# A build-time scheduler gets new prices for transfers and instructions, and its order of all instructions is searched anew

## The chip, the cores and the metric

The kernel runs on one core of a Trainium2 chip. The metric is the device time of one execution in microseconds (us). The median of three runs of the kernel before is 364.08 us (363.77 to 364.1).

## The reference

Block-sparse attention and then a SoLU feed-forward layer, all in float32.

```python
# q, k, v: 4 batches, 8 heads, 768 positions, 64 columns
k_sum = k in blocks of 32, max;  v_sum = v in blocks of 32, mean
scores = [q k^T / 8 where |i-j| < 16, else -1e9 ;  q k_sum^T / 8 + log 32]
a = softmax(scores);  x = a @ [v; v_sum]          # 3072 tokens x 512 (heads side by side)
h = x @ w_in                                      # 512 -> 1024
solu = h * softmax(h);  ln = layernorm(solu) * g
out = ln @ w_out                                  # 1024 -> 512
```

## The kernel before

The 3072 tokens are 24 tiles of 128 (`t`), two to a step of attention (256 positions of one batch, in two halves of four heads each). For one half, `scores` makes score products on TensorE (tile `s`), VectorE adds the mask and takes the maximum (L678), ScalarE makes the exponentials (L686), VectorE or GpSimd scales them (`MUL_E`, tile `e`); `values_turn` transposes them on TensorE (tile `t`) and copies them to `at`; `values` multiplies with the value rows `vt` (tile `x`). Then `first` (tiles 0 to 7) or `first_two` (pairs from tile 8 on, seven products for eight) computes h (tiles `h`, `hu`, `hl`, `hf`), `solu` the activation, and `second_parts` the last product (tile `o`, 24 matmuls of 128x128 by 128x512 for each tile). All float32 products are made of three matmuls on rounded high and low parts, so nearly each operand costs VectorE, ScalarE or GpSimd a rounding and a subtraction. The weights arrive as 64-bit floats, and `rounded` turns each of 16 pieces (8 of `w_in`, 8 of `w_out`) into high and low words with five instructions (tile `cv`), the last of them an integer addition (`ADD_W`).

From tile 6 on, the centred rows are transposed by a trip through DRAM: `send` (L1038, L1042: tile `tbl`, one buffer, to `farl`) and `fetch` (L1048: four reads into `lt`).

Nothing is issued where it stands in the code. Each call of `op` hands a `Plan` one operation with its engines (one or a few to choose from), a price on each, what it reads and writes, and for a DMA its bytes. `Plan.order` then simulates the engines at build time: over and over it takes the operation that can begin first, ties by a due number, and puts it on the engine where it ends first. `Plan.issue` runs the operations in that order, and since every engine works its queue in order, this fixes the order on each engine. `SEARCHED` is a list of seeds; each shifts some due numbers or the leaning of some operations to an engine, and the list is what an earlier search kept. A price that differs from the chip's changes nothing but the order.

Two more things come from the plan's clock. Where the plan sees TensorE idle before 80 us (`FILL`), `keep_up` issues matmuls of zeros (L1300), one for each 0.22 us of plan time. And `order` models the port that VectorE and GpSimd share: an operation with `port=True` on VectorE waits in the plan until a GpSimd operation with a port has ended (`lock`), and the other way round (`held`).

A transfer of the plan before has one pipe with a rate by time (`RATES`: 205 GB/s up to 6.9 us, then 420, 365, 410), and lands 0.2 us behind it up to 50 us of plan time and 2.2 us behind it later (`LAND`, `LATE`). The first product with the rows of v for the block means (L546) has `late = LATE_ROWS`, 2.2 us, which is added to its start when zeros are filled in.

Of the kernel before, what the change touches and what calls it, by code (L numbers as in the profile page):

```python
# [17 lines left out]
AF = mybir.ActivationFunctionType  # L18
ALU = mybir.AluOpType
AX = mybir.AxisListType  # L20

P = 128
# [63 lines left out]
class Plan:  # L86
# [6 lines left out]
    RATES = (6.9, 205.0), (30.0, 420.0), (60.0, 365.0), (1e9, 410.0)  # L93
    SMALL, LATE = 40.0, 50.0
    LAND = 2.2
# [8 lines left out]
    SEARCHED = -856134719, -860457018, 52477149, 195803496, 905169564, -371301522, -289478668, -495083861, -295360282,\  # L104
# [145 lines left out]
    def order(self):  # L250

        ready, free, then, dma, held, lock = {}, {}, {}, 0.0, 0.0, 0.0
# [18 lines left out]
        def take(e):  # L271

            if e in then:
                return next(((begin(e, at), o) for at, o in ready[e] if o is then[e]), None)
            best = None
            for at, o in ready[e]:
                t = begin(e, at)
                if any(begin(f, at) + loss(f, o, t) < t + loss(e, o, t) for f in o.can if f != e):
# [7 lines left out]
            for at, y in ready[e]:  # L286
                s = begin(e, at)
# [8 lines left out]
        while len(order) < len(self.ops):  # L296
# [11 lines left out]
            if e == "dve" and o.port:  # L308
                held = o.end
            if e == "pool" and o.port:  # L310
                lock = o.end
            if o.nbytes:
# [3 lines left out]
                o.end = (own if e == "act" else dma) + (0.2 if dma < self.LATE else self.LAND)  # L316
# [19 lines left out]
def attn_then_solu(ctx: ExitStack, tc: tile.TileContext, q, k, v, vr, vb, w_in, w_out, g_ln, out):  # L336
# [11 lines left out]
    COPY_KS = ((pool, 0.35), (dve, 0.19))  # L348
    COPY_P = ((act, 0.48), (dve, 0.6))
    COPY_X = ((act, 0.48), (dve, 0.6))  # L350
    LO_W = ((dve, 0.6), (pool, 1.26))
    ADD_W = ((dve, 0.6), (pool, 1.3))
    MUL_E = ((pool, 1.8), (dve, 1.07))
# [91 lines left out]
    def rounded(key, tag, bufs):  # L445
# [19 lines left out]
        op(act, 0.6, lambda: nc.scalar.activation(  # L465
# [8 lines left out]
        tt(ADD_W, ALU.add, high, high, low, r=[(st, 1)], w=[(st, 0)], port=True)  # L474
# [77 lines left out]
    def mean_values_pe(b):  # L552
# [18 lines left out]
        for g in range(4):  # L571
            op(act, 0.34, lambda g=g: nc.scalar.dma_start(
# [53 lines left out]
    def scores(b, g, pp, direct=False, each=False):  # L626
# [38 lines left out]
        else:  # L665
            yield 2.0 if direct else 1.07, lambda: (mm(0), mm(1)), [(qs, 2 * pp), (qs, 2 * pp + 1)] + ([x, y] if direct else [kw]), [sc]
# [24 lines left out]
        op(act, 0.2, lambda: nc.scalar.activation(out=z.ap, in_=z.ap, func=AF.Copy, bias=1e-9), w=[z])  # L691
        op(dve, 0.1, lambda: nc.vector.reciprocal(out=z.ap, in_=z.ap), w=[z])
# [4 lines left out]
    def run(*parts, rest=True, off=0.0):  # L697
# [18 lines left out]
    def values_turn(b, g, pp):  # L716
# [4 lines left out]
        yield 0.62, lambda: turn_halves(tp.ap[:KC], lambda n: e.ap[:, n, :]), [e], [tp]  # L721
# [5 lines left out]
    def values(b, g, pp, t=NT, apart=False):  # L727
# [36 lines left out]
        yield 2.2 if apart else 1.17, mm, [vs, at] + [vm] * apart, [xb]  # L764
# [19 lines left out]
    def combine(b, g, pp, xb):  # L784
# [19 lines left out]
        half, whole = ((act, 0.34), (dve, 0.33)), ((act, 0.48), (dve, 0.6))  # L804
        lo_h, lo_w = [(dve, 0.33)], [(dve, 0.6)]
        lo_hs, lo_ws = [(dve, 0.33), (pool, 0.7)], [(dve, 0.6), (pool, 1.28)]
        if pp == 0:
# [4 lines left out]
            split(hi, lo, 1, 1, 0, lambda: of(1), [(f, 1)], (((act, 0.34), (dve, 0.2)), lo_hs))  # L812
        else:
# [8 lines left out]
            split(hi2, lo2, 2, 1, 0, lambda: of(2), [(f, 2)], (((act, 0.34), (dve, 0.2)), lo_hs))  # L822
# [79 lines left out]
    def first(t):  # L902
# [5 lines left out]
        for c, nh in sorted(w_in_pieces, key=lambda x: x[::-1]):  # L908
# [7 lines left out]
            op(pe, 0.695, mm, r=[(hi, c), (lo, c), w], w=[hp])  # L916
        solu(t, [(lambda hp=hp: hp.ap, hp) for hp in hs])

    def first_two(t, behind, turns, rest=True):
# [7 lines left out]
        def product(xs, n, w, to, first, after=()):  # L927
            hi, lo = xs
            for c in range(2):
# [5 lines left out]
                op(pe, 0.695, mm, r=[(hi, n), (lo, n), *w(c).keys], w=[to])  # L935
# [41 lines left out]
    def solu(t, hs, maxes=None):  # L977
# [16 lines left out]
        for i, (hp, key) in enumerate(hs):  # L994
            op(act, 0.71, lambda i=i, hp=hp: nc.scalar.activation(  # L995
# [350 lines left out]
```

## Time and profile before

| what | value |
|---|---|
| median of three runs | 364.08 us |
| span of the profiled execution (its own time is not given apart from the span) | 362.6 us |
| TensorE busy (matmul) | 354.2 us, 98% |
| VectorE, ScalarE, GpSimd busy | 84%, 78%, 43% |
| granted TensorE clock | 1.00 through the span |

The span is that of one profiled execution, from its first to its last instruction; the runs take 1.2 to 1.5 us more than it. A busy time of TensorE holds the zeros too, and the ends of matmuls are modelled, so 98% does not say that TensorE computes 98% of the time.

### The profile page before, as it was taken

What the parts mean: (1) busy time and instruction counts of PE and PEld (TensorE: products, weight loads), DVE (VectorE), ACT (ScalarE), POOL (GpSimd) and SP (SyncE); (2) the same over time, 40 slices, a digit from 0 to 9 for tenths busy, and PEclk for the clock granted to TensorE, in tenths of its full rate; (3) what the DMA queues carried; (4) which work ended last, traced back from release to release, by engine and by line L of the source; (5) the groups of instructions that cost most, each with busy time, mean ns of one, the idle gap of its engine ahead of it and who ended that gap; (6) DMA issues with size and microseconds to landing.
All of it is one profiled execution on the core that took longest, in us unless ns stands there. A gap on an engine that the chain in (4) does not pass through costs nothing.

```text
span 362.6 us, 9384 instructions
## 1 busy us (share of the span) xinstructions
PE 354.2 (98%) x3332; PEld 277.0 (76%) x3332; DVE 305.5 (84%) x964; ACT 281.6 (78%) x815; POOL 157.3 (43%) x290
## 2 busy tenths in 40 slices
PE   8999999999999998999999999999999999999995
PEld 3537667768777786788788888888888888888885
DVE  4989999998999999997899999797797996947430
ACT  4888999979869978989698696896796796946320
POOL 6612330166968867423924147350335054534200
PEclk9999999999999999999999999999999999999999
DMA  7999994145325435538489384384164283344611
GB/s 241 413 414 405 359 397 155 62 113 165 130 77 196 136 131 173 172 95 273 141 270 285 117 280 153 114 288 148 57 201 174 55 276 101 116 147 168 209 58 58
DMA packets 28530, 68.19 MB, mean 188 GB/s; under 512 B 3852, under 2 KB 13324, under 8 KB 26948
## 3 DMA queue, kind: packets, MB, share of 16 engines
q1 hardware_dynamic: 24620, 60.87, 49.6%
q10 hardware_dynamic: 3864, 6.74, 5.2%
q8 instruction: 26, 0.43, 0.5%
q14 instruction: 20, 0.16, 0.1%
HBM read 49.55 MB, written 15.73 MB: 180 GB/s over the span
## 4 chain that ended last, share of the span: by engine, by line
PE 63%; DVE 22%; DMA 5%; ACT 3%; SPq 3%; issue 2%; POOL 1%; ACTq 0%; DVEq 0%
PE o L1108 29%; PE hu L932 10%; PE hl L932 5%; PE x L761 4%; PE s L659 3%; PE h L913 3%; DVE e L678 3%; PE t L714 3%; DMA qt<-in_q 2%; DMA farl<-tbl 2%; PE hf L932 2%; DVE e L370 2%; SPq L602 2%; DVE w L489 2%; DVE hm L990 2%
## 5 line engine op out<-in xcount | busy, mean ns | idle before, releaser
L1108 PE MATMUL o<-w,lh 128*128 128x512 f32 (+1 forms) x400 | 128.0, 385 | 0.9 <-DVE w L489 0.9
L1108 PEld LDWEIGHTS o<-w,lh 128*128 128x128 f32 x400 | 74.1, 188 | 16.4 <-DVE w L489 1.2
L1108 PE MATMUL o<-w,ll 128*128 128x512 f32 (+1 forms) x200 | 76.2, 381 | 0.0
L686 ACT ACTIVATE e<-e,nm 128x120 f32<-128x120 f32 x192 | 73.2, 388 | 0.0
L913 PE MATMUL h<-w,xh 128*128 128x512 f32 x128 | 43.0, 400 | 0.0
L1108 PEld LDWEIGHTS o<-w,ll 128*128 128x128 f32 x200 | 37.6, 188 | 6.8
L678 DVE CUSTOM_DVE_ANT_0 e<-s,mask 128x120 f32<-128x120 f32 x192 | 40.6, 276 | 0.5 <-PE s L659 0.3
L686 ACT ACTIVATION_READ_ACCUMULATOR e<-e,nm 128x1 f32 x192 | 37.0, 193 | 0.0
L363 ACT COPY at<-t 120x512 f32<-120x512 f32 x43 | 22.9, 591 | 11.0 <-PE t L714 8.6
L913 PEld LDWEIGHTS h<-w,xh 128*128 128x128 f32 x128 | 24.0, 188 | 7.3 <-ACT at L363 0.8
L1015 ACT ACTIVATE he<-he,nmu 128x512 f32<-128x512 f32 x36 | 24.7, 721 | 4.4 <-DVE nmu L1006 4.3
L761 PEld LDWEIGHTS x<-at,vt 120*64 120x64 f32 (+1 forms) x768 | 24.4, 138 | 4.1 <-issue 2.6
L371 POOL TENSOR_TENSOR ll<-lt,lh 128x512 fp32r<-128x512 f32 x11 | 16.5, 1512 | 23.5 <-DVE lh L364 15.8
L1038 DVE STREAM_TRANSPOSE tbl<-he 128x1024 f32<-128x1024 f32 x18 | 22.3, 1239 | 5.3 <-DMA farl<-tbl 2.7
L1114 ACT ACTIVATE os<-o,y 128x512 f32<-128x512 f32 (+1 forms) x20 | 13.5, 675 | 17.0 <-PE o L1108 16.8
L761 PE MATMUL x<-at,vt 120*64 120x64 f32 (+1 forms) x768 | 26.5, 224 | 0.0
L588 POOL TENSOR_TENSOR st_v<-st_v 96x512 f32<-96x512 f32 (+3 forms) x28 | 22.1, 797 | 8.3 <-DMA st_v<-in_vb 7.8
L1018 ACT ACTIVATE sq<-he 128x1024 bf16<-128x1024 f32 x24 | 25.3, 1056 | 0.1
L913 PE MATMUL h<-w,xl 128*128 128x512 f32 x64 | 25.1, 393 | 0.3 <-DVE xl L770 0.3
L363 ACT CAST lh<-lt 128x512 fp32r<-128x512 f32 x33 | 19.2, 608 | 7.8 <-DMA lt<-farl 5.6
L995 ACT ACTIVATE he<-hs,hm 128x512 f32<-128x512 f32 x24 | 17.1, 716 | 8.3 <-DVE hm L985 8.3
L370 DVE TENSOR_TENSOR e<-e,z 128x960 f32<-128x960 f32 x18 | 23.1, 1281 | 0.1
(175 smaller groups left out, 836.0 us busy)
## 6 DMA issues: line engine op xcount, KB each, us to landing
vt<-in_v SPq DMA_DIRECT2D x12, 1024.0 KB
farl<-tbl SPq DMA_DIRECT2D x18, 512.0 KB
lt<-farl SPq DMA_DIRECT2D x72, 128.0 KB
kraw<-in_k SPq DMA_DIRECT2D x16, 400.0 KB
out<-os ACTq DMA_DIRECT2D x23, 256.0 KB
qt<-in_q SPq DMA_DIRECT2D x11, 512.0 KB
raw<-in_w_in SPq DMA_DIRECT2D x8, 512.0 KB
raw<-in_w_out SPq DMA_DIRECT2D x8, 512.0 KB
```

What stands on the lines that cost most here:

```text
L363: by = {act: lambda: nc.scalar.copy(out=to(), in_=of()), dve: lambda: nc.vector.tensor_copy(out=to(), in_=of()), pool: lambda: nc.gpsimd.t ...
L370: by = {dve: lambda: nc.vector.tensor_tensor(out=to(), in0=a(), in1=b(), op=kind), pool: lambda: nc.gpsimd.tensor_tensor(out=to(), in0=a() ...
L588: op(pool, 0.15 + w * 0.0021, lambda w=w, o=o: nc.gpsimd.tensor_tensor(out=o.ap[:n, :w], in0=x.ap[:n, :w], in1=x.ap[:n, w:2 * w], op=ALU.add),
L678: nc.vector.tensor_tensor_reduce(out=e.ap[:, n, :], in0=sc.ap[:, j, (2 * i + up) * KC:(2 * i + up + 1) * KC], in1=mask[:, mi, :], scale=-S ...
L686: nc.scalar.activation(out=e.ap[:, n, :], in_=e.ap[:, n, :], func=AF.Exp, bias=nm.ap[:, n:n + 1], scale=-1.0, accum_out=z.ap[:, n:n + 1])
L761: nc.tensor.matmul(xp()[j * D:(j + 1) * D, i, qs], vs.ap[:k, u, cs], at.ap[:k, u % 2, n[j] + u // 2, :], start=not apart, stop=not apart o ...
L913: nc.tensor.matmul(hp.ap, a.ap[:, c, ts], w.ap[:, i], start=(c == 0 and n == 0), stop=(c == NKC - 1 and n == 2))
L932: nc.tensor.matmul(to.ap, operand(y, n)[:, c], w(c).ap(i), start=first and c == 0 and k == 0, stop=c == 1 and k == 2, skip_group_check=True)
L1015: (act, 0.57, lambda sl=sl: nc.scalar.activation(out=e.ap[:, sl], in_=e.ap[:, sl], func=AF.Identity, bias=nmu.ap))], port=True)
L1018: op(act, 1.13, lambda: nc.scalar.activation(out=sq.ap, in_=e.ap, func=AF.Square, accum_out=ss.ap), r=[e], w=[sq, ss])
L1038: op(dve, 1.13, lambda: nc.vector.transpose(out=tb.ap.rearrange("p (q c a) -> p q c a", q=4, a=32), in_=of().rearrange("p (c q a) -> p q c ...
L1108: nc.tensor.matmul(o.ap[:, cols], a.ap[:, f, :], w.ap[:, i, cols], start=(f == 0 and n == 0), stop=(f == NFC - 1 and n == 2))
```

## The change

The prices of transfers and of some forty operations are replaced, at most eight transfers are under way in the plan, the port no longer couples VectorE's integer addition in `rounded` to GpSimd, and `SEARCHED` holds 151 new seeds in place of 105. The operations, their data and their dependencies stay; which of several engines takes an operation, and the order on each engine, queues of transfers included, follow from the new plan.

```diff
-    RATES = (6.9, 205.0), (30.0, 420.0), (60.0, 365.0), (1e9, 410.0)
-    SMALL, LATE = 40.0, 50.0
-    LAND = 2.2
+    RATES = (8.5, 330.0), (1e9, 412.0)
+    SMALL = 40.0
+    LAND = 1.0
+    SLIP = 17.0, 50.0, 0.9
+    RING = 8
-    SEARCHED = -856134719, -860457018, 52477149, 195803496, 905169564, -371301522, -289478668, -495083861, -295360282,\
...
+    SEARCHED = -664592949, -693925857, -701921031, -814109230, -697896537, -833220612, -117212915, -248144961,\
...
-        def begin(e, at):
-            return max(free.get(e, self.START), at)
+        def begin(e, at, o):
+            at = max(free.get(e, self.START), at)
+            return max(at, landed[-self.RING]) if o.nbytes and len(landed) >= self.RING else at
...
-            other = lock if e == "dve" and o.port else held if e == "pool" else 0.0
+            other = lock if e == "dve" and o.port is True else held if e == "pool" else 0.0
...
-            if e == "dve" and o.port:
+            if e == "dve" and o.port is True:
                 held = o.end
...
-                o.end = (own if e == "act" else dma) + (0.2 if dma < self.LATE else self.LAND)
+                o.end = (own if e == "act" else dma) + self.LAND + (self.SLIP[2] if self.SLIP[0] < dma < self.SLIP[1] else 0.0)
+                landed.append(o.end)
...
-    COPY_KS = ((pool, 0.35), (dve, 0.19))
+    COPY_KS = ((pool, 0.305), (dve, 0.19))
...
-    ADD_W = ((dve, 0.6), (pool, 1.3))
-    MUL_E = ((pool, 1.8), (dve, 1.07))
+    ADD_W = ((dve, 0.6), (pool, 1.23))
+    MUL_E = ((pool, 1.75), (dve, 1.07))
...
-        tt(ADD_W, ALU.add, high, high, low, r=[(st, 1)], w=[(st, 0)], port=True)
+        tt(ADD_W, ALU.add, high, high, low, r=[(st, 1)], w=[(st, 0)], port=pool)
...
-            yield 2.0 if direct else 1.07, lambda: (mm(0), mm(1)), [(qs, 2 * pp), (qs, 2 * pp + 1)] + ([x, y] if direct else [kw]), [sc]
+            yield 2.0 if direct else 0.98, lambda: (mm(0), mm(1)), [(qs, 2 * pp), (qs, 2 * pp + 1)] + ([x, y] if direct else [kw]), [sc]
...
-            op(pe, sum(cost) - 0.25 * (len(mine) - 1) - off, lambda: [f() for f in fns],
+            op(pe, sum(cost), lambda: [f() for f in fns],
...
-        yield 0.62, lambda: turn_halves(tp.ap[:KC], lambda n: e.ap[:, n, :]), [e], [tp]
+        yield 0.61, lambda: turn_halves(tp.ap[:KC], lambda n: e.ap[:, n, :]), [e], [tp]
...
-        yield 2.2 if apart else 1.17, mm, [vs, at] + [vm] * apart, [xb]
+        yield 1.9 if apart else 1.03, mm, [vs, at] + [vm] * apart, [xb]
...
-        op(sp, 0.43, lambda: nc.sync.dma_start(out=d.ap, in_=tb.ap), r=[tb], w=[d], nbytes=int(P * DF * 4 * FARK))
+        op(sp, 0.43, lambda: nc.sync.dma_start(out=d.ap, in_=tb.ap), r=[tb], w=[d], nbytes=P * DF * 3)
...
-                op(pe, 0.695 * k, mm, r=[hi, lo, wt[2 * NKC + f]], w=[o])
+                op(pe, 0.04 + 0.64 * k, mm, r=[hi, lo, wt[2 * NKC + f]], w=[o])
...
-                out=out[t * P:(t + 1) * P, cols], in_=os.ap[:, cols]), r=[os], nbytes=int(P * 2048 * k))
+                out=out[t * P:(t + 1) * P, cols], in_=os.ap[:, cols]), r=[os], nbytes=int(P * 205 * k))
...
-            parts = [run(scores(*step(t + i)), off=0.18) for i in (4, 5) if t + 4 < NT]
-            parts += [run(values(*step(t + i)), off=0.23 - 0.05 * (i - 2)) for i in (2, 3)]
+            parts = [run(scores(*step(t + i))) for i in (4, 5) if t + 4 < NT]
+            parts += [run(values(*step(t + i))) for i in (2, 3)]
```

The other new prices are of the same kind, a few hundredths of a microsecond each (0.71 to 0.68 for the exponential of h, 1.13 to 1.04 for its squares, 0.57 to 0.615 for the centring on ScalarE).

## Rows read from the trace of the kernel before

**Rows 1.** The page, part 1: the span, and busy time, share and instructions of each engine.

```profile
span 362.6 us, 9384 instructions
PE 354.2 (98%) x3332; PEld 277.0 (76%) x3332; DVE 305.5 (84%) x964; ACT 281.6 (78%) x815; POOL 157.3 (43%) x290
```

**Rows 2.** Busy time by stretch: the stretch and its length, then busy us (and instructions) of PE, PEld, DVE, ACT, POOL, the granted clock, the DMA share and GB/s.

```profile
26.00:80.00 54.00, 52.80 (x608) 37.99 (x605) 52.00 (x164) 48.81 (x137) 15.87 (x26) 1.00 0.71 259
80.00:174.00 94.00, 92.26 (x927) 74.51 (x925) 87.56 (x283) 81.20 (x249) 61.02 (x101) 1.00 0.47 157
174.00:359.00 185.00, 184.76 (x1591) 153.81 (x1585) 146.00 (x458) 133.12 (x380) 68.05 (x137) 1.00 0.50 162
...
30.00:80.00 50.00, 48.80 (x536) 35.05 (x532) 49.47 (x160) 45.31 (x131) 14.62 (x18) 1.00 0.69 247
```

**Rows 3.** What TensorE's matmuls waited for: us in total, times, longest.

```profile
PE o L1108 <- DVE w L489: 0.9, 1, 0.9
PE s L659 <- ACT at L363: 0.9, 1, 0.9
...
PE t L714 <- POOL e L371: 0.5, 1, 0.5
PE s L659 <- issue: 0.3, 1, 0.3
PE h L913 <- DVE xl L770: 0.3, 1, 0.3
```

**Rows 4.** TensorE in order of time: start, length, line, tile and shape, count. L1300 are the zeros.

```profile
15.28 4.92 PE L1300 MATMUL vs_ps<-zero 128*128 128x512 bf16 x22
20.13 5.33 PE L546 MATMUL vs_ps<-st_v,sel 128*24 128x512 f32 x12
...
43.17 1.47 PE L1300 MATMUL x<-zero 128*128 128x512 bf16 x6
...
64.61 1.47 PE L1300 MATMUL x<-zero 128*128 128x512 bf16 x6
...
75.35 0.39 PE L1300 MATMUL x<-zero 128*128 128x512 bf16 x1
...
77.45 0.61 PE L1300 MATMUL x<-zero 128*128 128x512 bf16 x2
```

**Rows 5.** The queue of SyncE: in order of time, the first loads of w_in, the last three of them ahead of the rows of v, and those; and from the view of its waits, what its loads of weights waited for.

```profile
0.79 0.41 SPq L442 DMA_DIRECT2D raw<-in_w_in  x1
...
5.71 4.07 SPq L442 DMA_DIRECT2D raw<-in_w_in  x3
10.29 2.32 SPq L534 DMA_DIRECT2D st_v<-in_vr  x3
...
SPq L442 <- DMA raw<-in_w_in: 8.3, 5, 3.4
```

**Rows 6.** Instructions of VectorE that GpSimd could take, in order of time, from 30 to 80 us: the first and the last of six additions of `rounded`, and the last of two scalings of `e`.

```profile
33.07 0.69 DVE L370 CUSTOM_DVE_ANT_0 cv<-cv 128x1024 uint16<-128x1024 uint16 x1
...
62.14 1.16 DVE L370 TENSOR_TENSOR e<-e,z 128x960 f32<-128x960 f32 x1
...
70.15 0.68 DVE L370 CUSTOM_DVE_ANT_0 cv<-cv 128x1024 uint16<-128x1024 uint16 x1
```

**Rows 7.** VectorE and GpSimd side by side, in order of time; the row of L489 with three numbers is from the view by tile (count, then shortest, median and longest ns).

```profile
53.16 0.76 POOL L1028 TENSOR_SCALAR ss<-ss 128x1 f32<-128x1 f32 x1
53.19 0.68 DVE L370 CUSTOM_DVE_ANT_0 cv<-cv 128x1024 uint16<-128x1024 uint16 x1
...
64.49 1.27 POOL L371 TENSOR_TENSOR cv<-cv 128x512 int32<-128x512 int32 x1 [10.14 <-DVE hz L998]
64.54 0.28 DVE L678 CUSTOM_DVE_ANT_0 e<-s,mask 128x120 f32<-128x120 f32 x1
...
72.20 1.29 POOL L371 TENSOR_TENSOR cv<-cv 128x512 int32<-128x512 int32 x1 [6.43 <-DVE cv L470]
72.81 1.24 DVE L489 SCALAR_TENSOR_TENSOR w<-cv,g_sb,w 128x512 fp32r<-128x512 f32 x1
74.24 1.79 POOL L371 TENSOR_TENSOR e<-e,z 128x960 f32<-128x960 f32 x1
...
L489 DVE SCALAR_TENSOR_TENSOR w<-cv,g_sb,w x8: 741/749/1944, 39.6 to 74.6; 128x512 fp32r<-128x512 f32 x8
...
335.50 0.19 POOL L1028 TENSOR_SCALAR ss<-ss 128x1 f32<-128x1 f32 x1
```

**Rows 8.** One turn of the stretch from 174 us on, from the chain of work that ended last: start, length, tile, matmuls.

```profile
198.26 1.09 PE t L714 x32
...
205.69 1.80 PE s L659 x64
207.49 2.02 PE x L761 x64
```

**Rows 9.** The last trip through DRAM and its use, in order of time: the store, the first rounding that waited for the reads, the last subtraction, and the first half-wide matmul of the last tile.

```profile
336.91 0.34 SPq L1042 DMA_DIRECT2D farl<-tbl  x1
...
343.69 0.62 ACT L363 CAST lh<-lt 128x512 fp32r<-128x512 f32 x1 [5.65 <-DMA lt<-farl]
...
348.19 1.46 DVE L370 TENSOR_TENSOR ll<-lt,lh 128x512 fp32r<-128x512 f32 x2
...
353.08 0.28 PE L1108 MATMUL o<-w,ll 128*128 128x256 f32 x1
```

More of the change, by code (lines that the diff above doesn't have):

```diff
@@ L250, in order @@
     def order(self):
-        ready, free, then, dma, held, lock = {}, {}, {}, 0.0, 0.0, 0.0
+        ready, free, then, dma, held, lock, landed = {}, {}, {}, 0.0, 0.0, 0.0, []
         for o in self.ops:
@@ L273, in take @@
             if e in then:
-                return next(((begin(e, at), o) for at, o in ready[e] if o is then[e]), None)
+                return next(((begin(e, at, o), o) for at, o in ready[e] if o is then[e]), None)
             best = None
             for at, o in ready[e]:
-                t = begin(e, at)
-                if any(begin(f, at) + loss(f, o, t) < t + loss(e, o, t) for f in o.can if f != e):
+                t = begin(e, at, o)
+                if any(begin(f, at, o) + loss(f, o, t) < t + loss(e, o, t) for f in o.can if f != e):
                     continue
@@ L286, in take @@
             for at, y in ready[e]:
-                s = begin(e, at)
+                s = begin(e, at, y)
                 if t < s and s - t < self.WAIT * (t + cost(e, o, t) - s) and y.due + self.FAR < best[1].due:
@@ L571, in mean_values_pe @@
         for g in range(4):
-            op(act, 0.34, lambda g=g: nc.scalar.dma_start(
+            op(act, 0.55, lambda g=g: nc.scalar.dma_start(
                 out=y.ap[WIN + 6 * g:WIN + 6 * g + 6, :], in_=rows.ap[32 * g:32 * g + 6, :]),
@@ L690, in scores @@
             op(act, 1.52, lambda i=i: exps(i), r=[nm], w=[(e, i), (z, i)])
-        op(act, 0.2, lambda: nc.scalar.activation(out=z.ap, in_=z.ap, func=AF.Copy, bias=1e-9), w=[z])
-        op(dve, 0.1, lambda: nc.vector.reciprocal(out=z.ap, in_=z.ap), w=[z])
+        op(act, 0.11, lambda: nc.scalar.activation(out=z.ap, in_=z.ap, func=AF.Copy, bias=1e-9), w=[z])
+        op(dve, 0.08, lambda: nc.vector.reciprocal(out=z.ap, in_=z.ap), w=[z])
         tt(MUL_E, ALU.mult, lambda: e.ap, lambda: e.ap,
@@ L695, in scores, with run @@
         es[b, g, pp] = e
-    def run(*parts, rest=True, off=0.0):
+    def run(*parts, rest=True):
         mine = [x for x in ((f, next(f, None)) for f in parts) if x[1]]
@@ L802, in wide @@
                 "p (k i c) -> p k i c", k=m, i=2)
-        half, whole = ((act, 0.34), (dve, 0.33)), ((act, 0.48), (dve, 0.6))
+        half, whole = ((act, 0.26), (dve, 0.33)), ((act, 0.473), (dve, 0.6))
         lo_h, lo_w = [(dve, 0.33)], [(dve, 0.6)]
@@ L915, in mm @@
                         stop=(c == NKC - 1 and n == 2))
-            op(pe, 0.695, mm, r=[(hi, c), (lo, c), w], w=[hp])
+            op(pe, 0.68, mm, r=[(hi, c), (lo, c), w], w=[hp])
         solu(t, [(lambda hp=hp: hp.ap, hp) for hp in hs])
@@ L1000, in solu @@
            w=[zs])
-        op(dve, 0.1, lambda: nc.vector.reciprocal(out=zs.ap[:, 0:1], in_=zs.ap[:, 0:1]), w=[zs])
+        op(dve, 0.07, lambda: nc.vector.reciprocal(out=zs.ap[:, 0:1], in_=zs.ap[:, 0:1]), w=[zs])
         for i, (hp, key) in enumerate(hs):
@@ L1014, in solu @@
                 out=e.ap[:, sl], in0=e.ap[:, sl], scalar1=nmu.ap, scalar2=None, op0=ALU.add)),
-                (act, 0.57, lambda sl=sl: nc.scalar.activation(
+                (act, 0.615, lambda sl=sl: nc.scalar.activation(
                     out=e.ap[:, sl], in_=e.ap[:, sl], func=AF.Identity, bias=nmu.ap))], port=True)
         sq = plan.buf(sb, [P, DF], BF16, "sq", 1, f"sq{t}")
-        op(act, 1.13, lambda: nc.scalar.activation(
+        op(act, 1.04, lambda: nc.scalar.activation(
             out=sq.ap, in_=e.ap, func=AF.Square, accum_out=ss.ap), r=[e], w=[sq, ss])
-        mul = lambda to, x: op(pool, 0.3, lambda: nc.gpsimd.tensor_tensor(out=to.ap, in0=to.ap, in1=x.ap, op=ALU.mult), r=[x], w=[to])
+        mul = lambda to, x: op(pool, 0.26, lambda: nc.gpsimd.tensor_tensor(out=to.ap, in0=to.ap, in1=x.ap, op=ALU.mult), r=[x], w=[to])
         op(pool, 0.3, lambda: nc.gpsimd.tensor_scalar(
             out=ss.ap, in0=ss.ap, scalar1=1.0 / DF, scalar2=1e-6, op0=ALU.mult, op1=ALU.add), w=[ss])
-        op(pool, 0.46, lambda: nc.gpsimd.tensor_tensor(out=y.ap, in0=ss.ap, in1=mhalf, op=ALU.pow),
+        op(pool, 0.52, lambda: nc.gpsimd.tensor_tensor(out=y.ap, in0=ss.ap, in1=mhalf, op=ALU.pow),
            r=[ss], w=[y])
@@ L1027, in solu @@
         mul(ss, y)
-        op(pool, 0.3, lambda: nc.gpsimd.tensor_scalar(
+        op(pool, 0.15, lambda: nc.gpsimd.tensor_scalar(
             out=ss.ap, in0=ss.ap, scalar1=-0.5, scalar2=1.5, op0=ALU.mult, op1=ALU.add), w=[ss])
@@ L1037, in send @@
         tb = plan.buf(sb, [P, DF], F32, "tb", 1, f"tb{name}")
-        op(dve, 1.13, lambda: nc.vector.transpose(
+        op(dve, 1.16, lambda: nc.vector.transpose(
             out=tb.ap.rearrange("p (q c a) -> p q c a", q=4, a=32),
@@ L1067, in rows_split @@
             of = lambda r=r: lt.ap.rearrange("p i (c a) -> p c i a", a=32)[:, 4 * r:4 * r + 4]
-            copy(((act, 0.48), (dve, 0.34)), lambda part=part: part(hi), of, r=[lt], w=[(hi, r)], port=True)
+            copy(((act, 0.508), (dve, 0.335)), lambda part=part: part(hi), of, r=[lt], w=[(hi, r)], port=True)
             tt(LO_W, ALU.subtract, lambda part=part: part(lo), of, lambda part=part: part(hi).bitcast(F32),
@@ L1257, in turns @@
             steps = [i for i in (t + 2, t + 3) if i < NT and i != PAIRED + 2]
-            chain([run(values_turn(*step(i)), off=0.1 if i < steps[-1] else 0.0) for i in steps])
+            chain([run(values_turn(*step(i))) for i in steps])
         behind = second_parts(t - 4 - (t > LATER))
@@ L1281, in attn_then_solu @@
             second(t - 3)
-            chain([run(turn(t - 2), off=0.09), run(turn(t - 1), off=0.14)])
+            chain([run(turn(t - 2)), run(turn(t - 1))])
         if 0 < b < B - 1 and g < 2:
```

20 lines of the change are left out of this document (10 added, 10 removed), and 30 rows, old and new, of the table SEARCHED.

## The prediction

> **What bounds the kernel now.** I read the busy times first, then the same by stretch, then TensorE's waits, and last TensorE in order of time, since its busy time hides matmuls of zeros. TensorE is at 98% with VectorE at 84% [rows 1]. From 174 to 359 us TensorE is busy 184.76 of 185 us, with VectorE at 79% and GpSimd at 37% [rows 2]. No order of the same matmuls makes that stretch shorter; a new one can only open holes in it. From 26 to 80 us VectorE is busy 52.0 of 54 us and GpSimd only 15.9 [rows 2]: there VectorE is the limit, and TensorE's 52.8 us hold zeros. So what an order can win lies ahead of 174 us, and it has two sizes.
>
> From 26 to 80 us the plan filled 15 zeros in four places (6, 6, 1 and 2) [rows 4]. A zero takes 0.22 us: 22 of them lie between 15.28 and 20.13 us [rows 4]. So 15 x 0.22 = 3.3 us, plus the idle times that the zeros did not cover, 0.9 us for the weights w of VectorE and 0.3 us for xl [rows 3]: 4.5 us. From 80 to 174 us no zeros are issued, and the idle times are 0.9 us (for a copy of at), 0.5 us (for e from GpSimd) and 0.3 us [rows 3]: 1.7 us. Together 6.2 us, 1.7% of the time, is all that a better order behind the first 26 us can take out.
>
> **The change part by part.** No operation is added or taken away, so each term is a move of work between engines or in time.
>
> *VectorE's work ahead of 80 us.* From 30 to 80 us VectorE is free for 0.5 us of 50 [rows 2]. A hole of TensorE goes there only if work leaves VectorE. GpSimd is free for 50 - 14.6 = 35.4 us [rows 2] and could take six additions and two scalings [rows 6]. From start to start these cost VectorE 0.60 and 1.07 us by the plan, 0.68 and 1.16 us by the rows with the overlap of the next: 6 x 0.60 + 2 x 1.07 = 5.7 us. GpSimd needs 1.27 and 1.79 us for them [rows 7]: 6 x 1.27 + 2 x 1.79 = 11.2 us, which it has. But GpSimd's work costs VectorE something. Beside the two GpSimd operations from 72.2 to 76.0 us, two instructions of L489 took 1.24 and 1.94 us instead of 0.74 [rows 7], 1.7 us lost for 3.8 us of GpSimd's time, or 0.45 us for one. At that price all eight moves lose 11.2 x 0.45 = 5.0 us and net 0.7 us. Beside an instruction that reads its scores from PSUM nothing is lost: L678 takes 0.28 us under a GpSimd addition, its usual time [rows 7]. So the term lies between 0 and the whole 4.5 us. The new prices make GpSimd 0.05 to 0.07 us cheaper and let the addition stand beside GpSimd, both in the direction of more work there. I take half, -2.25 us, since a plan can place some moves beside L678 and some not.
>
> *The holes from 80 to 174 us.* 1.7 us in all; they are late copies and scalings, small differences between plan and chip, which prices nearer to the rows should halve: -0.85 us (bounds 0 and -1.7).
>
> *The zeros ahead of the first rows of v.* These can be counted from the code. Ahead of the rows stand twelve transfers, six pieces of w_in of 524,288 bytes (one first, the last three just ahead) [rows 5], four key parts of 409,600 and two query parts of 262,144. With the old rates the second query part lands at 14.87 us of plan time, its scores end at 17.22, and the rows land at 19.86; zeros run until 19.86 + 2.2 (`late`), which makes 4.84 / 0.22 = 22 of them, just what the trace has [rows 4]. With the new rates the same transfers land at 13.55 and 19.54 us (with `SLIP`), the scores end at 15.91, and `late` is still 2.2: 5.83 / 0.22 makes 27. On the chip the first product would start not at 20.13 but at 15.28 + 27 x 0.22 = 21.2 us: +1.1 us. If the holes behind it take this up, it costs 0; if the search lets the rows of v load ahead of the three pieces of w_in (4.07 us of issue [rows 5]), it turns into a gain of up to the 4.85 us that the zeros fill now. I take +1.1, the only figure that the code itself gives.
>
> *Eight transfers under way.* The chip holds to this already: SyncE's loads of weights waited 8.3 us for earlier loads to land [rows 5], so the order of issue stays that of landing. At nothing: the data moves at the same rate. If it were not hidden, the 8.3 us would be the cover that is gone, but they are there now.
>
> *Prices of TensorE.* In the stretch from 174 us, the new plan pays for two transposes, scores and values 2 x 0.61, 2 x 0.98 and 2 x 1.03 us, where the chip takes 1.09, 1.80 and 2.02 [rows 8]: 0.33 us too much a turn, 2.6 us in eight turns. The trip through DRAM becomes 3.5 us shorter in the plan (the store loses 1.1 us of moving and 1.2 of landing, the reads 1.2 of landing). In the trace the last subtraction ends at 348.19 + 1.46 = 349.65 us and its first matmul is at 353.08 [rows 9], 3.4 us of slack, so about as much as goes. I cost both at nothing, because that slack covers them; what it costs without it is a rival below. Prices of the output's bytes and the small new prices of ScalarE and VectorE only move the plan's own end and ties: nothing, hidden behind TensorE's 184.76 us.
>
> **The sum.** -2.25 - 0.85 + 1.1 = -2.0 us. The span of 362.6 us [rows 1] becomes 360.6; the median of 364.08 us, 1.5 us above that span, becomes 362.1 us.
>
> **The rule that speaks against it.** The new plan says that VectorE's integer addition and GpSimd do not hold each other up. One pair of rows bears on it: a GpSimd instruction on one column, 0.19 us elsewhere, took 0.76 us beside such an addition of 0.68 us [rows 7]. The Trainium skill (SBUF — State Buffer, section SBUF: two separate sides) has the port pair of VectorE and GpSimd as an exclusive lock, taken also by a VectorE instruction with two SBUF inputs, and this addition has two. The trace agrees with that.
>
> **The rivals.**
>
> *The holes only move.* VectorE stays full, the moves to GpSimd lose what they win (0.7 us net, above), other holes open: 0 to -0.7 us, 364.1 us. For it speaks that 15 zeros stand where the old plan knew of a hole and its search left it; against it that GpSimd is free two thirds of that time.
>
> *More than half goes.* All 6.2 us, and the first rows without loss: 364.1 - 6.2 = 357.9 us at the most, some 359.5 as a middle. Against it: it needs all VectorE moves to be free of loss.
>
> *The late stretch opens (slower).* With 2.6 us of TensorE's time too much and 3.5 us of the trip taken out, the plan may bring rounded rows or `at` just in time by its own clock, which is late on the chip. One hole as large as the largest now, 0.9 us [rows 3], in half of eight turns is 3.6 us: -2.0 + 3.6 = +1.6, so 365.7 us. It decides from 2.0 us of holes behind 174 us on. Against it: VectorE has 39 us free there [rows 2].
>
> *Additions hold GpSimd (slower).* Each of the rounded pieces' additions that the plan sets beside GpSimd costs it 0.57 us (0.76 - 0.19) that the plan does not know. Were nine of them in front of something that TensorE waits for, 5.1 us would come on top of -2.0: 367.2 us; from four on it is no gain. Against it: of all holes now only 0.5 us wait for GpSimd [rows 3].
>
> **How the numbers follow.** The forecast, one half of the holes gone: 0.53, by itself 360.4 to 363.3 us. More than half: 0.12. Holes that only move: 0.14. The late stretch: 0.14. Additions: 0.07. A measurement of this kernel can tell about 0.2%, 0.73 us, from no change. The forecast and the second rival are faster: 0.65; the first rival is the same: 0.14; the two others are slower: 0.21. The range of 8 in 10 goes from 360.0 to 365.8 us: it leaves out most of the second rival (0.09) and, above, the last and the worse part of the late stretch (0.1).
>
> **What would show it.** Right: fewer than 15 zeros between 26 and 80 us, more GpSimd time there than 15.9 us with VectorE still full, holes from 80 to 174 us below 1.7 us, and the stretch behind solid. The start: 27 zeros ahead of the product with the rows of v, if the loads keep their order. Wrong: idle time of TensorE behind 174 us, waits of TensorE for e, kw or ll from GpSimd, or as many zeros as now in other places. What would upset the prediction most is another order of the first loads, which sets all of the first 30 us.

## The result, and the profile after

The kernel after is slower: 367.4 us by the median of four runs (366.3 to 370.3) against 363.9, a ratio of 1.011 (95% interval 1.0071 to 1.0149). Its runs spread over 4 us, those of before over 0.4. The profiled execution took 366.33 us, the least of the four, with a span of 364.6. Two executions stand outside all times below: one of e6 at a granted clock of 0.756 (438 us, the one of its profile), and one of e15 of 1970 us.

The page, part 1, and busy time by stretch (columns as in [rows 2]), after:

```profile
PE 355.1 (97%) x3333; PEld 276.5 (76%) x3333; DVE 294.0 (81%) x950; ACT 279.3 (77%) x813; POOL 176.9 (49%) x306
```

```profile
26.00:80.00 54.00, 52.62 (x587) 37.36 (x589) 52.03 (x165) 46.75 (x133) 22.59 (x28) 1.00 0.69 250
80.00:174.00 94.00, 94.00 (x948) 75.77 (x939) 83.34 (x277) 82.77 (x252) 72.61 (x119) 1.00 0.51 166
174.00:361.00 187.00, 184.61 (x1597) 152.96 (x1595) 138.10 (x446) 134.20 (x383) 70.29 (x136) 1.00 0.49 158
...
26.00:53.00 27.00, 27.00 (x365) 19.74 (x367) 25.75 (x84) 24.05 (x70) 14.34 (x21) 1.00 1.00 378
53.00:80.00 27.00, 25.62 (x234) 17.62 (x228) 26.28 (x81) 22.69 (x64) 8.25 (x8) 1.00 0.39 122
```

Against [rows 2]: from 80 to 174 us TensorE, which had been idle for 1.7 us, is now solid; from 26 to 80 us GpSimd works 22.6 instead of 15.9 us and VectorE is as full as before; behind 174 us, where TensorE had missed 0.24 us, it misses 2.39. What TensorE waited for behind 80 us, and where (timeline):

```profile
PE x L773 <- DVE hx L954: 1.7, 1, 1.7
...
PE o L1120 <- ACT os L1126: 0.5, 1, 0.5
```

```profile
14.59 6.00 PE L1312 MATMUL vs_ps<-zero 128*128 128x512 bf16 x27
20.52 3.61 PE L558 MATMUL vs_ps<-st_v,sel 128*24 128x512 f32 x8
...
74.92 2.12 PE L1312 MATMUL x<-zero 128*128 128x512 bf16 x9
...
86.66 0.50 PE L925 MATMUL h<-w,xh 128*128 128x512 f32 x1
...
235.14 1.15 PE L773 MATMUL x<-at,vt 120*64 120x64 f32 x32 [1.65 <-DVE hx L954]
...
243.81 0.50 PE L1120 MATMUL o<-w,lh 128*128 128x512 f32 x1 [0.49 <-ACT os L1126]
```

**Cutting both traces at the same work.** A lag by the clock mixes up what is slower with what is merely in another order. Both kernels hold the same 1876 operations, and in the two plans' orders the first 397 are the same set, and the first 1080 again. There the traces can be compared exactly, by the start of TensorE's last operation of the set:

| operations | before | after | difference |
|---|---|---|---|
| first 397 | 85.11 us | 86.66 us | +1.55 |
| next 683 | 119.06 (to 204.17) | 116.67 (to 203.33) | -2.39 |
| rest, to the last matmul | 154.43 (to 358.60) | 157.65 (to 360.98) | +3.22 |

The sum is +2.38 us. The spans of these two executions differ by 2.0 us (362.6 and 364.6), since before takes 0.4 us more behind the start of its last matmul. TensorE's holes make 2.39 of the 3.22 us of the rest; for the other 0.8 no row here shows a cause.

**The place at 219 to 235 us.** SyncE's queue and VectorE, in order of time, after:

```profile
219.50 2.30 SPq L614 DMA_DIRECT2D vsum<-vacc  x3
221.90 0.46 SPq L1054 DMA_DIRECT2D farl<-tbl  x1
222.41 6.35 SPq L614 DMA_DIRECT2D vsum<-vacc  x5
228.87 1.86 SPq L1060 DMA_DIRECT2D lt<-farl  x4
```

```profile
233.60 0.76 DVE L376 CAST lh<-lt 128x512 fp32r<-128x512 f32 x2 [4.73 <-PE x L773]
234.40 0.68 DVE L954 CUSTOM_DVE_ANT_0 hs<-hl,hs 128x512 f32<-128x512 f32 x1
```

In its plan the four reads `lt<-farl` go out right behind eight small stores `vsum<-vacc`. On the chip the stores start late, behind the landing of `vt<-vsum`, cost 0.72 us each to issue (0.43 in both plans), and the seventh waits for an output store (two rows of SyncE's waits):

```profile
SPq L614 <- DMA vt<-vsum: 3.9, 1, 3.9
SPq L614 <- DMA out<-os: 2.6, 1, 2.6
```

So the reads go out at 228.87 us and land until 233.1. Set against the plan of after, VectorE's last reduction ahead of the casts starts 7.7 us later than planned (227.93 for 220.18), the first store 9.7 and the reads 14.7. Of the 7 us between, about 2 come from `vt<-vsum`, which landed 4.7 us after its issue instead of 2.9, 2.4 from issuing the stores, and 2.6 from the wait for the output store, which landed after 4.7 us instead of 3.1. The reads themselves land 2.7 to 2.8 us after their issue, sooner than the 2.9 to 3.2 of the plan. VectorE, which the plan has casting those rows first, stands idle for 4.73 us, and the addition to `hs` behind the casts, which frees the bank for `x`, comes late: TensorE's hole of 1.65 us.

### The profile page after: what moved, and what is told of

It reads as the page before. It is cut to its first block, busy times and chain, and to the rows that moved or that the text cites. A ratio compares the mean times of both kernels' runs of the same rounds, so it can differ in the third digit from the quotient of the medians.

```text
span 364.6 us, 9405 instructions
## 1 busy us (share of the span) xinstructions
PE 355.1 (97%) x3333; PEld 276.5 (76%) x3333; DVE 294.0 (81%) x950; ACT 279.3 (77%) x813; POOL 176.9 (49%) x306
## 4 chain that ended last, share of the span: by engine, by line
PE 82%; DVE 9%; DMA 5%; SPq 1%; ACT 1%; issue 1%; ACTq 0%; DVEq 0%
PE o L1120 34%; PE hu L944 12%; PE h L925 9%; PE hl L944 6%; PE x L773 6%; PE s L671 6%; PE t L726 3%; PE hf L944 3%; DMA vt<-in_v 3%; DMA qt<-in_q 2%; PE vs_ps L1312 2%; DVE he L1015 1%; PE vs_ps L558 1%; DVE e L690 1%; PE lt L726 1%
## 5 line engine op out<-in xcount | busy, mean ns | idle before, releaser
L383 POOL TENSOR_TENSOR ll<-lt,lh 128x512 fp32r<-128x512 f32 x13 | 18.0, 1388 | 39.8 <-DVE lh L376 21.6
L1023 POOL TENSOR_SCALAR he<-he,nmu 128x512 f32<-128x512 f32 x12 | 8.5, 712 | 34.0 <-DVE nmu L1018 34.0
L600 POOL TENSOR_TENSOR st_v<-st_v 96x512 f32<-96x512 f32 (+3 forms) x28 | 23.5, 849 | 1.5 <-DMA st_v<-in_vb 1.0
L1027 ACT ACTIVATE he<-he,nmu 128x512 f32<-128x512 f32 x29 | 20.0, 722 | 3.9 <-DVE nmu L1018 3.9
```

Source lines behind the costliest of these rows:

```text
L600: op(pool, 0.15 + w * 0.0021, lambda w=w, o=o: nc.gpsimd.tensor_tensor(out=o.ap[:n, :w], in0=x.ap[:n, :w], in1=x.ap[:n, w:2 * w], op=ALU.add),
L1027: (act, 0.615, lambda sl=sl: nc.scalar.activation(out=e.ap[:, sl], in_=e.ap[:, sl], func=AF.Identity, bias=nmu.ap))], port=True)
```

## The experiments

Times are medians; the ratio is to before on the same chip. Expectations stand as they were written ahead of each run.

**1. The two orders crossed at 1080.** The list of the other order takes the place of the tail:

```diff
         order = self.order()
+        order = order[:1080] + [mine[int(x[:-1])] for x in tail]   # number and engine of each operation
+        for o, x in zip(order[1080:], tail):
+            o.engine, (o.cost, o.fn) = names[x[-1]], o.can[names[x[-1]]]
```

> The first 1080 operations in the order of the kernel after (until about 203 us), the other 796 in the order of the kernel before, each on the engine that its own order gives it. Theory 'late jam' (all that is lost is lost at 219 to 245 us, behind SyncE's queue; the first 200 us of after are 0.9 us ahead of before): 363.0 us, 0.9 below before, with 27 zeros at the start and no hole of VectorE of 4 us at 229 us. Rival 'early loss' (the profile of after is its fastest run, and what makes the median slower lies in its first 200 us: the late start, more additions on GpSimd, new prices): 366 us or more.

Measured: 364.59 us (363.4 to 366.5), 1.0016 (0.9997 to 1.0034). Between the two theories: its lowest times, 363.4, are those of the late jam, but its profile has a hole of 0.8 us at 170 us, which the profile of after had not.

> The reverse: the first 1080 operations in the order of before, the other 796 in that of after. Theory 'late jam': 363.9 + 3.3 = 367.2 us (after lost 3.3 us against before from 200 us to its end), with x waiting for VectorE's hs near 235 us. Rival 'early loss': 364 us, as before.

Measured: 366.06 us (365.6 to 366.7), 1.006 (1.0048 to 1.0073). The last stretch of after costs 2.0 us by itself, with the casts at 232.67 us behind 3.65 us of idle VectorE. Less than 3.2, and with a quarter of after's spread, where e1, with after's first 200 us, has 3.1 us of it: most of the spread comes from ahead of 200 us.

**2. The place at 219 to 235 us mended**, in after (e3) and behind the first 1080 operations of before (e12, where the stores alone are moved):

```diff
+        # e3 and e12: the eight vsum<-vacc behind the four lt<-farl of rows 12
+        # e3 only: the addition to hs ahead of the two casts lh<-lt
+        for ahead, moved in moves:
+            for n in moved:
+                order.remove(mine[n])
+            at = order.index(mine[ahead])
+            order[at:at] = [mine[n] for n in moved]
```

> After, with two things moved near 219 to 235 us: the eight small stores vsum<-vacc are issued behind the four reads lt<-farl of row group 12 instead of ahead of them, and VectorE adds hs ahead of the two casts lh<-lt instead of behind them. Theory 'late jam': the holes of TensorE at 235 and 243 us (1.65 and 0.5 us) go, the reads are issued near 223 instead of 229 us, and the time is that of after less 2.2 us, 365.2 by the median. Rival 'early loss': same as after, 367.4. Rival 'the wait only moves' (the next reads or the rows of v come late instead): a hole of 1 us or more at 235 to 260 us, 366 to 367.4.

> After unchanged, for the spread of its times on the same chip beside the others. Its four runs lay between 366.3 and 370.3 us, those of before within 0.4 us. Theory 'late jam': 366 to 370 again, and a slower run than the profiled one shows longer holes at 226 to 245 us and nothing else. Rival 'early loss': the slower run shows its extra time ahead of 200 us.

Measured together: e3 365.87 us (364.8 to 366.8), after again 368.39 us (366.1 to 369.1). The two moves win 2.5 us, and the holes at 235 and 243 us are gone (one of 0.5 us now stands at 202 us). The profile of after again (366.1 us of span, 1.5 more than the first) shows both effects side by side:

```profile
PE x L773 <- DVE hx L954: 1.6, 1, 1.6
PE hu L944 <- DVE xl L382: 1.1, 1, 1.1
PE o L1120 <- ACT os L1126: 0.5, 1, 0.5
```

The late holes are as in the first profile; the middle row, at 171 us, is new. So much of the level is set late, and the spread early: each theory had one half.

> First 1080 operations in the order of before, the rest in that of after (366.06 us without more), and of that rest one thing moved: the eight stores vsum<-vacc are issued behind the four reads lt<-farl of row group 12; VectorE's order stays (casts ahead of its addition). Theory 'queue of SyncE' (the stores, slowed by the eight transfers that may be under way, hold up the reads, and the casts on VectorE hold up hs): reads near 223 us, VectorE idle under 1 us ahead of the casts, no hole of TensorE at 234 and 242 us, 364.6 us. Rival 'VectorE's order' (the casts ahead of the addition are the cause, late reads or not): 365.5 or more, with the hole at 234 us.

Measured: 364.40 us, 1.0013 (1.0004 to 1.0023), 1.66 us less than e2. SyncE and VectorE of this run:

```profile
223.06 3.45 SPq L1104 DMA_DIRECT2D lt<-farl  x4
226.56 6.12 SPq L658 DMA_DIRECT2D vsum<-vacc  x8
```

```profile
230.23 0.76 DVE L420 CAST lh<-lt 128x512 fp32r<-128x512 f32 x2 [1.10 <-PE o L1164]
231.03 0.68 DVE L998 CUSTOM_DVE_ANT_0 hs<-hl,hs 128x512 f32<-128x512 f32 x1
```

With VectorE's order unchanged, earlier reads alone take 3.65 us of idle time down to 1.10 and close both holes. So in this order SyncE's late reads open them. They do not by themselves: in before the same reads go out nearly as late, at 227.88 us, behind the same eight stores, and TensorE has no hole, for there VectorE adds to `hs` ahead of the cast. SyncE and VectorE of before:

```profile
221.63 6.13 SPq L602 DMA_DIRECT2D vsum<-vacc  x8
227.88 1.86 SPq L1048 DMA_DIRECT2D lt<-farl  x4
```

```profile
228.09 0.69 DVE L942 CUSTOM_DVE_ANT_0 hs<-hl,hs 128x512 f32<-128x512 f32 x1 [1.25 <-PE hl L932]
...
232.55 0.42 DVE L364 CAST lh<-lt 128x512 fp32r<-128x512 f32 x1
```

What is new in after is the pair: reads that come late, and an addition that the plan sets behind them. No run moves the addition alone.

**3. The middle alone, and its hole at 169 us.** `order[397:1080]` of before is replaced by after's.

> Operations 397 to 1079 in the order of after (about 86 to 203 us), all others in that of before. At 397 and at 1080 both orders have done the same set of operations, so the profiles of before and after can be cut there: TensorE ends the first 397 at 85.11 in before and 86.66 in after (+1.55), the next 683 in 119.06 and 116.67 us (-2.39), the rest in 153.8 and 157.0 us (+3.2). Theory 'three stretches' (each order takes its own time in each stretch, whatever stands ahead): 364.0 - 2.4 = 361.6 us, up to 362.9 where the hole of 0.8 to 1.3 us at 169 to 171 us comes, which three of four profiles of after's order have; faster than both kernels. Rival 'borrowed' (the middle of after is quick only since its first stretch did more ahead of it, buffers and transfers): 364 us or more, with holes right behind 86 us.

Measured: 362.21 us (361.5 to 363.0), 0.9945 (0.9926 to 0.9964): faster than both kernels, by 1.7 us where the cut said 2.4, less the hole. "Borrowed" falls. Against e1 (364.59 us), from which it differs in the order of the first 397 operations alone, it is 2.4 us faster: after's first stretch costs that much by these two runs (1.55 by the cut). The profile of e5 has the hole, of 1.1 us. There VectorE and GpSimd meet; after (first profile) and e1, VectorE and GpSimd of each:

```profile
165.49 1.25 DVE L1050 STREAM_TRANSPOSE tbl<-he 128x1024 f32<-128x1024 f32 x1 [0.46 <-ACT hs L375]
...
168.58 0.69 DVE L382 TENSOR_TENSOR xl<-sums,xh 128x512 fp32r<-128x512 f32 x1
...
168.67 3.16 POOL L600 TENSOR_TENSOR st_v<-st_v 96x512 f32<-96x512 f32 x3
```

```profile
165.61 1.25 DVE L1106 STREAM_TRANSPOSE tbl<-he 128x1024 f32<-128x1024 f32 x1 [0.56 <-ACT hs L431]
...
168.71 1.91 DVE L438 TENSOR_TENSOR xl<-sums,xh 128x512 fp32r<-128x512 f32 x1
...
168.75 2.99 POOL L656 TENSOR_TENSOR st_v<-st_v 96x512 f32<-96x512 f32 x3
```

About a tenth of a microsecond between the starts goes with whether the subtraction takes 0.69 or 1.91 us. The Trainium skill (SBUF — State Buffer, section SBUF: two separate sides) has an exclusive lock on a port pair between GpSimd and a VectorE instruction with two SBUF inputs. The subtraction has two, and the trace agrees, with the 1.2 us of a wait for one sum of GpSimd. Which of the two had the pair first these start times do not tell: in e1 the subtraction stands 0.04 us ahead of the sums and is the one that waits.

In after again (e4) and in e5 the transpose itself comes late:

```profile
167.32 1.25 DVE L1050 STREAM_TRANSPOSE tbl<-he 128x1024 f32<-128x1024 f32 x1 [2.08 <-ACT e L698]
```

```profile
164.00 1.25 DVE L1080 STREAM_TRANSPOSE tbl<-he 128x1024 f32<-128x1024 f32 x1 [1.02 <-DMA farl<-tbl]
```

`tbl` is one buffer: the transpose waits until the store of the rows before it has landed. Taking the last update of the store's semaphore as its landing, the transpose starts 0.12 to 0.13 us behind it in all six profiles with after's middle (165.36 and 165.49 us in after, 167.19 and 167.32 in e4, 163.88 and 164.00 in e5). This one store took 5.35 to 6.97 us from issue to landing in them; after's plan has 3.67. Between the two profiles of after this store makes 1.6 us, about as much as their times differ (366.33 and 367.90 us). The slowest executions, up to 370.3 us, have no profile, so what makes the rest of the 4 us of spread is not shown.

> As the run before it, and GpSimd's ten sums of the last rows of v (st_v3_1, L600 of after, between 160 and 179 us), which nothing needs ahead of 219 us, are put into its idle time at 181 to 186 and 190 to 193 us. Theory 'no margin' (the hole at 170 us comes when the first of these sums waits for its rows of v and holds up GpSimd's addition, or when the sum takes the port 0.1 us ahead of VectorE's xl, which then takes 1.9 instead of 0.7 us): no hole at 169 to 171 us in the profile, 361.6 us, and a spread under 1 us. Rival 'the wait is elsewhere': same time and spread as the run before it.

> The middle of after with the first and last stretch of before, and GpSimd's ten last sums of rows of v put into its idle time in two portions: five (3.9 us) at 181 us, ahead of the additions of he10 and he11, and five (1.9 us) at 190 us. With seven sums in the first portion (5.0 us for a gap of 5.1) it took 362.4 us, in 10 of 11 runs within 362.0 to 363.2. Theory 'no margin': without the hole at 169 us, and with 1 us of room ahead of he10, 361.6 us, spread under 1 us. Rival 'the wait is elsewhere': 362.2 or more, and the profile shows TensorE waiting behind 170 us for another thing.

Measured: e6 362.4 us, nearly all runs within 0.4 us, e11 361.94 us (361.75 to 362.87), 0.9949 (0.9937 to 0.9962), which the intervals do not tell from e5. In e11's profile, of its longest execution, the subtraction takes 0.69 us again, but a hole of 0.6 us stays, since the store landed after 6.5 us and the transpose waited for it. The sums were one of two causes of the hole; the landing is the other. Taking the sums away narrowed the spread (1.4 us in e5) and won nothing in the median that these runs can tell.

**4. The accounting without the searches.** `for seed in self.SEARCHED` becomes `for seed in ()`; then the new prices of operations and the new accounting of transfers are each taken alone.

> Before without its list of seeds: the order as the old prices and rules alone give it. In its own plan TensorE ends at 359.4 us (355.0 with the search), 4.4 us later. If the search of before is real on the chip: about 368.4 us. If searching only fits the plan: 364 to 366.

> After without its list of seeds: the order as the new prices and the rule of eight transfers alone give it. In its own plan TensorE ends at 354.8 us (349.6 with the search). Theory 'the search lost it' (new prices and rule are sound, the new search fitted the plan's gaps): no more than 367.4 + 1, and below the unsearched before by 1 us or more. Rival 'the accounting lost it' (new prices make worse orders): slower than the unsearched before by 2 us or more. Where after's search is real, 367.4 + 5.2 = 372.6 us.

> The kernel before without its seeds, with the new accounting of transfers alone (rates, landing, eight under way, what a transfer costs to issue and its bytes); prices of operations as before. Its own plan ends TensorE at 359.8 us, against 359.4 with the old transfers. Unsearched before took 369.95, unsearched after 372.86 us. Theory 'prices' (the cheaper prices of operations, TensorE's above all, make the worse order): 370 or less. Theory 'transfers' (the rule of eight and the new landings make it): 372 to 373.

> The reverse: the kernel after without its seeds, with the old accounting of transfers and the new prices of operations. Its own plan ends TensorE at 353.4 us. Theory 'prices': 372 to 374. Theory 'transfers': 370 or less. Were the plan right, 364.

Unsearched, before takes 369.95 us and after 372.86: both searches are real on the chip (6.0 and about 5 us), and it is the accounting that lost. Of it, "prices" falls: the prices alone take 368.03 us, less than either, and the transfers alone 375.87. So the transfers' part was split again: e13 sets `RING = 10 ** 6`; e14 keeps `RING = 8` with the rates, landings, bytes and issue prices of before. These four are together called landings below; the new port rule is among the prices. Before's own median is 363.8 to 364.0 us beside all of these runs.

> The kernel after without its seeds and without the rule that at most eight transfers are under way in the plan; new prices, rates and landings stay. With the rule it took 372.9 us, with the old transfers altogether 368.0. Theory 'landings' (transfers are planned to land earlier than the plan of before had it, 1.0 instead of 2.2 us behind their bytes, an output store of 512 columns 3.1 instead of 8.9 us, and orders made on that have no slack for a late one): 372 to 374. Theory 'rule of eight' (the rule itself makes the worse orders): 368 to 369.5.

> The kernel after without its seeds: new prices of operations, the old rates, landings, bytes and issue prices of transfers, and the rule of eight under way. Theory 'landings': 368 to 369.5. Theory 'rule of eight': 372 or more.

Measured, in us (the ratio is to before, with its interval; idle is TensorE from 174 to 356 us):

| unsearched order | prices | landings | rule of eight | TensorE's end in its plan | median | ratio | idle |
|---|---|---|---|---|---|---|---|
| e7 (before) | old | old | no | 359.4 | 369.95 | 1.016 (1.0141 to 1.0179) | 0.61 |
| e10 | new | old | no | 353.4 | 368.03 | 1.0115 (1.0101 to 1.0128) | 0.93 |
| e14 | new | old | yes | 355.5 | 369.87 | 1.0162 (1.0149 to 1.0175) | 1.09 |
| e9 | old | new | yes | 359.8 | 375.87 | 1.0344 (1.0323 to 1.0364) | 4.24 |
| e8 (after) | new | new | yes | 354.8 | 372.86 | 1.0257 (1.0208 to 1.0306) | 2.97 |
| e13 | new | new | no | 355.5 | 373.61 | 1.0268 (1.0227 to 1.031) | 3.85 |

The last column is read from rows like these, of e10 and of e8:

```profile
80.00:174.00 94.00, 92.51 (x951) 74.01 (x952) 87.76 (x281) 82.82 (x251) 67.54 (x111) 1.00 0.47 157
174.00:356.00 182.00, 181.07 (x1555) 148.16 (x1555) 146.54 (x457) 134.93 (x387) 63.41 (x127) 1.00 0.51 166
```

```profile
80.00:174.00 94.00, 90.26 (x925) 72.17 (x924) 80.19 (x266) 81.16 (x249) 67.44 (x111) 0.98 0.47 156
174.00:356.00 182.00, 179.03 (x1545) 146.47 (x1544) 142.57 (x459) 134.30 (x384) 65.18 (x130) 1.00 0.52 163
```

The three orders on new landings take 372.9 to 375.9 us and are idle for 3.0 to 4.2 us behind 174 us; the three on old ones 368.0 to 369.9 us and 0.6 to 1.1 us. The new landings by themselves cost 5.6 us without the rule of eight (e10 to e13) and 3.0 us with it (e14 to e8). Not all of that lies behind 174 us: of the 4.8 us from e10 to e8, TensorE is idle for 2.0 us more there and for 2.25 us more from 80 to 174 us. The new prices, all taken together, win 1.9 us (e7 to e10) and 3.0 us (e9 to e8). The rule of eight by itself is +1.8 us (e10 to e14) or -0.7 (e13 to e8): one order each, so its sign stays open, and a difference of 2 us between two single orders shows little by itself. And the plan's own end says nothing: e9 and e7 differ in it by 0.4 us and on the chip by 5.9.

How landings can do it shows in the plan's and the chip's times of the same transfers behind 85 us in before and after, from the issue to the last update of the transfer's semaphore:

| transfer | count | plan of before, chip | more than 1 us late | plan of after, chip | more than 1 us late |
|---|---|---|---|---|---|
| `farl<-tbl` | 18 | 5.8, 3.4 | 1 | 3.4, 3.8 | 8 |
| `lt<-farl` | 72 | 4.3, 3.0 | 3 | 3.1, 3.5 | 16 |
| `out<-os` | 25 | 10.1, 2.1 | 0 | 3.1, 2.4 | 8 |
| `vt<-vsum` | 8 | 4.5, 4.3 | 1 | 2.9, 4.2 | 6 |

(medians in us; the plan of before lets an output store move at 40 GB/s, the new one counts a tenth of its bytes). The new plan is nearer to the medians, except for `vt<-vsum`, and below them for three of the four kinds. So 38 of these 123 transfers landed over 1 us late by it, 5 by the old one, and a late transfer can meet work that has no room for it, as at 219 to 235 us. That this makes the holes of the unsearched orders too is argued, not shown: ahead of the largest one of e8 behind 174 us, 2.2 us that end at 206.09, VectorE had waited 2.8 us for a result of GpSimd by its profile, and not for a transfer.

**5. The good half, searched anew.** New prices, old transfers, and a short search of my own (14 seeds; e16: 16 seeds, with the rule of eight).

> New prices of operations, old transfers altogether, and a search of its own (14 seeds, by when TensorE ends in the plan: 353.4 to 349.5 us). Unsearched it took 368.0 us. The search of before won 4.4 us in its plan and 6.0 on the chip, that of after 5.2 and 5.0. Theory 'landings' (what lost was the transfers' part of the change): 363 to 364, faster than after by 3 us or more, with TensorE's holes behind 174 us under 1 us. Rival 'searches fit the plan' (any search on the tighter prices gives orders without slack): 366 or more.

> New prices, old landings and rates, the rule of eight, and a search of its own (16 seeds; TensorE ends in the plan at 355.5 unsearched, 351.3 us searched). Theory 'landings': 363 to 365, holes behind 174 us under 1 us. Theory 'rule of eight': 367 or more.

Measured: e15 362.43 us (361.6 to 363.1), 0.996 (0.9947 to 0.9973), with TensorE idle for 0.18 us of the same 182. It is faster than before by 0.4% and than after by 5.0 us, below what was expected of it. So the tighter prices can make a better order where transfers keep their slack. e16 took 366.93 us, above "landings" and at the edge of "rule of eight"; it is idle for 1.05 us behind 174 us. With another search behind it, it doesn't settle the rule; but it is as slow as after with the old landings, so that the rule of eight took part in what after lost is not excluded.

## Why the prediction was wrong

The forecast was 362.1 us, faster; the time is 367.4. Of its signs, more GpSimd time, the closed holes from 80 to 174 us and the 27 zeros came; fewer zeros from 26 to 80 us did not, and the stretch behind 174 us opened. By the cut, the first stretch was forecast at -1.15 us (-2.25 and +1.1) and took +1.55, the middle -0.85 and took -2.39, the last stretch nothing and took +3.22. So two steps failed, the transfers behind the cut and VectorE's work ahead of it:

- **The transfers at nothing: the trip through DRAM ("that slack covers them") and the output's bytes.** This step failed, with 3.2 us behind operation 1080. It looked at the slack of one trip, the last [rows 9]. At 219 to 235 us the slack was gone: the order of stores and reads there made 1.7 us (e2 to e12), with the reads 7 us later against VectorE than the plan had them. In unsearched orders the new landings cost 5.6 and 3.0 us (e10 to e13, e14 to e8), so the accounting of transfers is where the change loses. Which part of it made the other 1.5 us of after is not shown.
- **"Eight transfers under way: at nothing".** It went by the issue order of the first loads [rows 5]. Whether it held stays open: the rule costs 1.8 us and wins 0.7 in unsearched orders, and the searched order with it is slow (e16).
- **The rival "the late stretch opens"** named the stretch. Its chance was 0.14 and its condition, 2.0 us of holes, was met with 2.4, but it blamed TensorE's prices along with the trip. With the new prices and the old transfers no such holes come (e15, 0.18 us).
- **VectorE's work ahead of 80 us, -2.25.** This step failed too, in its sign: +1.55 us for the first 397 operations, all that lies ahead of the cut (2.4 by e1 and e5). Its holes were counted a little short, since the trace of before has three more zeros at 26.01 to 26.45 us, 18 in all from 26 to 80 us; after has 21. GpSimd takes three more integer additions, six instead of three between 26 and 77 us, and one scaling of `e` fewer, one instead of two. By the work done until then TensorE is 2.4 us ahead of before at 53 us. By 86 us it has given that back and 1.55 more, in zeros and holes ahead of the last weights. The largest group is the nine zeros at 74.92 us, ahead of the first of these matmuls at 77.15. VectorE and GpSimd ahead of it, after:

```profile
73.41 1.58 DVE L382 CUSTOM_DVE_ANT_0 cv<-cv 128x1024 uint16<-128x1024 uint16 x1
...
76.37 1.40 DVE L501 SCALAR_TENSOR_TENSOR w<-cv,g_sb,w 128x512 fp32r<-128x512 f32 x2
```

```profile
73.14 1.29 POOL L383 TENSOR_TENSOR cv<-cv 128x512 int32<-128x512 int32 x1 [4.34 <-ACT cv L477]
```

  VectorE's integer addition begins beside one of GpSimd's and takes 1.58 us, where the trace of before has 0.69 by the mean of eight. It is the pair that the new plan holds to be free of each other, and that the port rule weighed in the prediction has as locked: the trace bears the rule out, at 0.9 us for this pair. VectorE has no idle time from there to the scaling of the last weights, so that starts that much later, and the matmul follows its first half by 0.04 us. So work done earlier won nothing, while VectorE, as full as before, still set when the weights were ready. This is read from the trace; no run gives the old port rule back by itself.
- **The holes from 80 to 174 us, -0.85.** Right in sign, too small: -2.39 us to operation 1080 in the first profile, 0.8 to 1.3 less where the hole at 169 us comes.
- **27 zeros, +1.1.** The count was exact, 14.59 to 20.52 us. The cost was 0: the first h starts at 32.17 us against 32.10, since the products behind took it up.
- **Prices of TensorE, at nothing.** Not tried alone. The new prices of all operations together win 1.9 and 3.0 us in unsearched orders, so they are not what lost.
- **"Additions hold GpSimd".** The lock is real, but where it cost TensorE time it worked the other way: GpSimd held VectorE, once at 73.41 us (0.9 us) and, in some executions, in the subtraction at 169 us (1.2 us). Nine such cases, as that rival had them, were not there.
- **The medians.** "Span plus 1.5 us" held within 0.3 us (364.6 and 366.33), but no step asked how much of the order hung on a single transfer's landing. After spreads over 4 us, of which one store's landing shows 1.6, and its median is 1.1 us above the profiled run.

## What to carry to other kernels

Where a plan's price decides how much room a transfer gets, look at its late landings and not at the median alone: by prices nearer to the median 38 of 123 transfers landed over 1 us late here, and the orders made on them were the slower ones. Judge an order by the chip, and compare two orders where both have done the same set of operations, since such cuts also show which stretches to splice (here 361.9 us, faster than both). When a price table changes, take its parts alone on an order without the search; the search hides which part is sound. One order for each part is little, so try each in more than one setting.

## What the runs showed of the hardware

- In the trace SyncE's and ScalarE's transfers use the same eight semaphores, and of all 218 transfers none in before or after uses one again ahead of the last update of the transfer before on it. So a 6 KB store on SyncE's queue waited at 227 us for an output store of ScalarE's queue, issued at 222.54 us and landed at 227.27, although 15 of its 16 updates had come by 225.5 us.
- Issuing a store of 6 KB into a few rows takes SyncE 0.71 to 0.78 us in after, a store of 512 KB 0.32 to 0.47 us, mostly 0.34.
- The same store of 512 KB, in the six profiles with after's middle stretch, lands 5.35 to 6.97 us after its issue.
